# Part of the w2 gradient made between two passes: eight row blocks taken out of the background work of pass 4

## The chip, the cores and the metric

The kernel runs on one core of one Trainium2 chip. The metric is device time in microseconds (us); the program is one launch with one core, so the slowest core is that core. The time before is the median of three runs. The profile is of one further execution, which has its own time.

## The reference

Two layers of a decoder step are applied twice with the same weights: attention of one query token over a long key and value cache (A), then a dense layer with a squared relu (B). The kernel computes the output and its gradient with respect to the nine inputs but `B_x`. All tensors are bf16.

```python
# A: x is (1, 1, 1024); caches (1, 4, 65536, 128); wq (1024, 4096); wo (4096, 1024)
q = (x @ wq) as 32 heads of 128;  8 heads share one of 4 cache groups
p = softmax(q . k * 128**-0.5);   o = p . v;   return o @ wo
# B: w1 (1024, 3584), w2 (3584, 1024)
h = x @ w1 + b1;  r = max(h, 0);  g = r * r;  return g @ w2 + b2

x = x + A(layernorm(x));  x = x + B(layernorm(x))      # layers 1 and 2
x = x + A(layernorm(x));  x = x + B(layernorm(x))      # layers 3 and 4
out, vjp = jax.vjp(f, A_x, A_k_cache, A_v_cache, A_wq, A_wo, B_w1, B_b1, B_w2, B_b2)
return out, *vjp(grad_out)
```

There is only one token, so each weight gradient is a sum of two outer products, one per use of the weight. The gradient of w2 (`out_8`, 3584 x 1024) is

```python
grad_w2 = outer(L4.g, grad_out) + outer(L2.g, dx2)     # rank 2
```

where `L4.g` and `L2.g` are the squared relus of layers 4 and 2 and `dx2` is the gradient that reaches the output of layer 2. It is 28 row blocks of 128 rows.

## The kernel before, in words

**Passes.** The two caches are 64 MB each and are read in four passes: pass 1 (forward of layer 1), pass 2 (forward of layer 3), pass 3 (first backward of layer 3: its dq), pass 4 (both layers' gradients of k and v and the dq of layer 1). In the code they are `attn_fwd` with 0 and 1, `attn_bwd3` with 2 and `attn_bwd4` with 3. A pass is a list of items in `ITEMS`, 256 in each, each 8 columns of 128 cache rows of one of the four groups. `pipeline` (L846) runs its stages over the items with fixed lags. In pass 4 the stages `vT` and `vS` (transposes of v, scores L1390, product L1411) run up to 16 iterations ahead of the others, so its first 16 iterations hold only them.

**The arena.** `ARENA` is one SBUF tile of 20 granules of 1 MB (`GRAN`, L268). Eight of them hold the exponentials of the two forward passes during pass 3 and the start of pass 4. The other twelve are handed out by `take_one` (L292) when a `Slot` is made: cache halves of 1 MB (`kv8`, L351), weight slabs (`slabs`, L441) and output staging all come from there. Free granules carry the time at which they were given back; outside of pass 4 a request takes the one that has been free for longest, or, for output staging, the latest one that has been free for a pipeline step. A slot that was given back with `stored=True` counts as free five steps later. In pass 4 some granules are a ring, `RING`, for output staging; loads take granules outside of it. `xs` is a slot in which pass 4 keeps the products X of its first group, one half of 32 columns in each eighth, the last eighth first. Pass 3 keeps seven turned v halves for pass 4.

**Queues.** All loads go out on SP's queue (L361, L366, L458) and all stores on POOL's. An instruction that reuses a granule waits until the transfer or the engines that used it are done. PE, DVE and ACT run their instructions in the order in which the program lists them inside `tc.manual_schedule` (the turn is such a block); elsewhere, and between these instructions, the scheduler that builds the program orders them.

**The turn between pass 3 and pass 4** (L1854 to L1965). Four matrix-vector products follow from each other: `dn_job` (the last group through wq, gives `dx2`), `dh_job` (through w2, gives `dh2`), `dx_job` (through w1, gives `dx1`) and `do_job` (the first group of pass 4 through wo, gives dO). `rows.tra` turns a weight tile on PE (L688) and evicts it with ACT (kind `kta`) or DVE (`kt`); `rows.back` (L715) multiplies the turned tiles with the vector (L722); `rows.dot` does a tile on DVE instead (L677). `wo_part` turns four of the eight wo rows; it is called once ahead of the last `back` of `dx_job` and once inside its finish. The turned wo rows are written over the slab. When the last `back` of a job is done, `did` runs the job's finish; `dO_finish` (L952) makes the numbers with which the first scores of pass 4 start. Before, nothing of any weight gradient is made here.

**PSUM.** Up to here the pool `psA` has `ps_tr` (three buffers), `ps_sc` (two), `ps_mv`, `ps_bg` and `ps_acc`. Pass 4 opens `ps4`, where `ps_gg` (two buffers of 1024 columns) is for the outer products, and `ps_sc` has one buffer.

**The weight gradients** are background work of pass 4. `Background.step` (L792) is called once an iteration and advances the oldest generator in `bg.normal` by one step whenever `bg.done` is behind `bg.total * i / bg.steps`. `i` counts from the end of the 16 iterations ahead, and is 0 in these. The first generator is `g_outer` (L1537) for w2. Its first step turns the two columns of the right side into two rows (`rows2`, L1489); then, for each four row blocks, one step makes the rows of the left side and four steps make 128x1024 results with `rank2` (L1506) into a staging slot `og`, which is stored as 1 MB behind the last.

`evac` (L150) evicts PSUM with ACT or DVE; for kinds `f32` and `bf` it takes the engine that its running counters find less loaded, and the counters start at zero at pass 4.

Of the kernel before, what the change touches and what calls it, by code (L numbers as in the profile page):

```python
# [16 lines left out]
P = 128  # L17
# [3 lines left out]
def kernel(  # L21
# [24 lines left out]
    nc = tc.nc  # L46
# [47 lines left out]
    def ps_gg():  # L94
        return PS["pool"].tile([P, 1024], F32, name="ps_gg", tag="gg", bufs=2)
# [336 lines left out]
    def d_cols(ap, nb):  # L432
        return ap[:, nb * P:(nb + 1) * P]
# [1052 lines left out]

    def rows2(cols, halves, rows, f=False):  # L1489

        cc = tmp.tile([P, 2, 4, 2], BF, name="r2_cc")
        pg = ps_gg()
        for h, j0 in enumerate(halves):
            for l in range(2):
                nc.vector.tensor_copy(out=cc[:, h, :, l], in_=cols[l][:, j0:j0 + 4])  # L1495
            for jj in range(4):
                nc.tensor.matmul(pg[64 * h:64 * h + 2, jj * P:(jj + 1) * P], lhsT=cc[:, h, jj, :], rhs=ident_b[:, :],  # L1497
                                 start=True, stop=True, tile_position=(0, 64 * h))
        for h in range(len(halves)):
            r = slice(64 * h, 64 * h + 2)  # L1500
            if f:
                evac(rows[r, :].rearrange("r (p j) -> r p j", j=4), pg[r, 0:512].rearrange("r (j p) -> r p j", j=4), kind="f32")
            else:
                evac(rows[r, :], pg[r, 0:512], kind="f32")

    def rank2(out, lhs, rhs):  # L1506

        n = out.shape[1]
        pg = ps_gg()
        for h in range(n // 512):  # L1510
            r = slice(64 * h, 64 * h + 2)
            nc.tensor.matmul(pg[:, 512 * h:512 * h + 512], lhsT=lhs(r), rhs=rhs(r), start=True, stop=True, tile_position=(64 * h, 0))  # L1512
        evac(out, pg[:, 0:n], kind="f32")

    def g_outer_last(pool, out_dram, a_cols, b_cols, c0):

# [17 lines left out]
                yield  # L1534
            sl.free(stored=True)

    def g_outer(pool, out_dram, nA, nB, a_cols, b_cols, c0=0, a_f=False):  # L1537

        rb = pool.tile([66, 4 * P], BF, name="rowb", tag="rowb")
        rows2(b_cols, (0, 4), rb)  # L1540
        yield
        for a0 in range(0, nA, 4):
            ra = pool.tile([66, 4 * P], BF, name="rowa", tag="rowa", bufs=2)
            rows2(a_cols, (a0, a0), ra)
            yield
            sl = Slot("og", True)
            og = sl.t[:, :].rearrange("p (j n) -> p j n", j=4)
            for j in range(4):
                rank2(og[:, j, :], lambda r: d_cols(ra[r, :], j) if a_f else f_cols(ra[r, :], j), lambda r: rb[r, :])
                if j < 3:  # L1550
                    yield
            nc.gpsimd.dma_start(out=out_dram[a0 * P:(a0 + 4) * P, c0:c0 + 1024].rearrange("(p j) n -> p j n", j=4), in_=og)
            sl.free(stored=True)
            yield

# [501 lines left out]
```

## Time and profile before

| | us |
|---|---|
| median of three runs | 1936.69 (1935.64 to 1938.51) |
| the profiled execution | 1936.17 |
| its span in the profile | 1934.3 |
| DMA: bytes and mean rate over the span | 787.62 MB, 407 GB/s |
| of these: loads on SP's queue, stores on POOL's | 617.65 MB, 165.70 MB |
| the turn in the trace: last wq issue to the end of dO | 1095 to 1172 |
| pass 4 in the trace | 1171 to 1934 |

The profile's page gives each engine's busy time, then the span in 40 slices with a digit for the busy tenths of each engine and of the 16 DMA engines. The windows give the same for stretches of one's own choice, the granted PE clock, the share of the DMA engines that was busy and the bytes that they moved. A DMA issue in the timeline is the moment at which the queue handed the transfer over, not its end. A wait names the instruction that stood, the one that released it, and how long the engine had nothing to do; in the lists of waits this is the total, the count and the longest.

### The profile page before, as it was taken

What the parts mean: (1) busy time and instruction counts of PE and PEld (TensorE: products, weight loads), DVE (VectorE), ACT (ScalarE), POOL (GpSimd) and SP (SyncE); (2) the same over time, 40 slices, a digit from 0 to 9 for tenths busy, and PEclk for the clock granted to TensorE, in tenths of its full rate; (3) what the DMA queues carried; (4) which work ended last, traced back from release to release, by engine and by line L of the source; (5) the groups of instructions that cost most, each with busy time, mean ns of one, the idle gap of its engine ahead of it and who ended that gap; (6) DMA issues with size and microseconds to landing.
All of it is one profiled execution on the core that took longest, in us unless ns stands there. A gap on an engine that the chain in (4) does not pass through costs nothing. (4 is left out here: it accounts for less than half of the span.)

```text
span 1934.3 us, 66768 instructions
## 1 busy us (share of the span) xinstructions
PE 1576.4 (81%) x30099; PEld 1292.1 (67%) x30099; DVE 1172.2 (61%) x2448; ACT 1043.8 (54%) x1619; POOL 142.4 (7%) x325
## 2 busy tenths in 40 slices
PE   6878778678878878978787878888996987787977
PEld 6878777678777878867677875555654554454544
DVE  5645555255555554645464576777876886676766
ACT  3434334245333535446363465766876785576765
POOL 0000000000000000000000002111211211121211
PEclk9989999799999988998999999898988998798997
DMA  9999999999999999999999997999999999899998
GB/s 393 427 427 424 429 428 416 399 420 412 428 425 428 428 422 330 379 425 429 426 420 426 405 348 298 425 420 387 424 424 413 420 425 423 349 423 397 425 422 321
DMA packets 107148, 787.62 MB, mean 407 GB/s; under 512 B 9440, under 2 KB 16622, under 8 KB 42222
## 3 DMA queue, kind: packets, MB, share of 16 engines
q1 hardware_dynamic: 82782, 617.65, 77.3%
q0 software_dynamic: 24080, 165.70, 20.5%
q8 instruction: 235, 3.85, 0.7%
q14 instruction: 51, 0.42, 0.1%
HBM read 617.62 MB, written 165.69 MB: 405 GB/s over the span
## 5 line engine op out<-in xcount | busy, mean ns | idle before, releaser
L164 DVE COPY kt<-ps_tr 128x1024 bf16<-128x1024 bf16 x736 | 505.8, 688 | 427.1 <-PE ps_tr L1030 239.5
L161 ACT CAST arena<-ps_gg 128x1024 bf16<-128x1024 f32 x457 | 444.2, 1011 | 183.2 <-PE ps_gg L1434 132.4
L1030 PE MATMUL ps_tr<-ident_b,arena 128*128 128x128 bf16 x3840 | 308.4, 225 | 48.0 <-DMA arena<-in_A_k_cache_dram 35.3
L161 ACT COPY kt<-ps_tr 128x1024 bf16<-128x1024 bf16 x180 | 188.6, 1054 | 184.5 <-PE ps_tr L1224 107.2
L164 DVE CAST arena<-ps_gg 128x1024 bf16<-128x1024 f32 (+2 forms) x186 | 222.4, 1196 | 80.1 <-PE ps_gg L1434 36.0
L1030 PEld LDWEIGHTS <-arena 128*128 128x128 bf16 x3840 | 231.8, 101 | 56.7 <-DMA arena<-in_A_k_cache_dram 37.8
L1434 PE MATMUL ps_gg<-GG,xt 64*128 64x512 bf16 x1024 | 209.8, 408 | 51.2 <-DVE arena L164 36.7
L1131 PE MATMUL ps_acc<-arena 128*128 128x64 bf16 (+4 forms) x4096 | 204.6, 197 | 46.1 <-DMA arena<-in_A_v_cache_dram 33.7
L1048 PE MATMUL ps_sc<-L_qpad,kt 128*128 128x64 bf16 (+7 forms) x3584 | 182.6, 194 | 23.1 <-issue 11.7
L1353 PE MATMUL ps_tr<-ident_b,arena 128*128 128x128 bf16 x1824 | 178.1, 232 | 28.5 <-DMA arena<-in_A_v_cache_dram 25.7
L1113 ACT ACTIVATE arena<-S_sb,L_negm 128x128 bf16<-128x128 f32 x256 | 165.3, 1006 | 57.2 <-DVE L_negm L1098 43.6
L1224 PE MATMUL ps_tr<-ident_b,arena 128*128 128x128 bf16 x2032 | 161.7, 224 | 40.6 <-DMA arena<-in_A_v_cache_dram 39.1
L1131 PEld LDWEIGHTS <-arena 128*128 128x128 bf16 x4096 | 160.0, 101 | 52.1 <-DMA arena<-in_A_v_cache_dram 37.7
L1353 PEld LDWEIGHTS <-arena 128*128 128x128 bf16 x1824 | 117.6, 103 | 84.7 <-issue 54.2
L1048 PEld LDWEIGHTS <-kt 128*128 128x128 bf16 x3584 | 152.0, 100 | 27.3 <-issue 12.8
L1224 PEld LDWEIGHTS <-arena 128*128 128x128 bf16 x2032 | 122.6, 100 | 46.0 <-DMA arena<-in_A_v_cache_dram 41.7
L1465 PEld LDWEIGHTS <-arena 128*128 128x128 bf16 x2048 | 92.4, 101 | 56.4 <-issue 38.5
L1434 PEld LDWEIGHTS <-xt 64*128 64x128 bf16 x1024 | 64.4, 94 | 97.8 <-issue 60.2
L1113 ACT ACTIVATION_READ_ACCUMULATOR arena<-S_sb,L_negm 128x1 f32 x256 | 128.2, 501 | 0.0
L584 ACT ACTIVATE mv_t<-mv_t 128x1024 bf16<-128x1024 bf16 x96 | 102.0, 1064 | 43.0 <-DVE mv_t L595 42.8
L1278 PE MATMUL ps_acc<-dsT,arena 128*128 128x64 bf16 (+7 forms) x2048 | 102.4, 194 | 12.4 <-DMA arena<-in_A_k_cache_dram 7.2
L1390 PE MATMUL ps_sc<-DOB,kt 128*128 128x64 bf16 (+3 forms) x1824 | 112.3, 197 | 0.1
(319 smaller groups left out, 2104.3 us busy)
## 6 DMA issues: line engine op xcount, KB each, us to landing
arena<-in_A_k_cache_dram SPq DMA_DIRECT2D x82, 2048.0 KB, 21.3
arena<-in_A_v_cache_dram SPq DMA_DIRECT2D x79, 2048.0 KB, 20.1
out_dram<-arena POOLq DMA_DIRECT2D x149, 1024.0 KB, 15.6
arena<-in_A_v_cache_dram SPq DMA_DIRECT2D x84, 1024.0 KB, 13.1
arena<-in_A_k_cache_dram SPq DMA_DIRECT2D x84, 1024.0 KB, 14.6
arena<-in_A_wo_dram SPq DMA_DIRECT2D x22, 1024.0 KB, 14.9
arena<-in_B_w_dram SPq DMA_DIRECT2D x21, 1024.0 KB, 10.0
arena<-in_A_wq_dram SPq DMA_DIRECT2D x18, 1024.0 KB, 13.4
```

The costliest lines, as they stand in the source:

```text
L161: nc.scalar.copy(out=out, in_=in_)
L164: nc.vector.tensor_copy(out=out, in_=in_)
L584: nc.scalar.activation(out=t[:, :], in_=t[:, :], func=ACTF.Copy, accum_out=y[:, kc:kc + 1])
L1030: nc.tensor.transpose(pt[:, i, :], kb8[:, i, :], ident_b[:, :])
L1048: nc.tensor.matmul(state["ps_s"][:, s:s + w, :].rearrange("p a b -> p (a b)"), lhsT=kt[:, i, :], rhs=L["qpad"][:, g, 0:w, :].rearrange("p ...
L1113: nc.scalar.activation(out=E(p, g, c0, SU)[:, :, h], in_=S[:, h, :], func=ACTF.Exp, bias=L["negm"][:, g, su, h:h + 1], scale=SCALE, accum_ ...
L1131: nc.tensor.matmul(ps_o[:, 0:w, :], lhsT=vb8[:, i, :], rhs=E(p, g, c, w), start=(c % SU == 0), stop=(c % SU == SU - 1), skip_group_check=True)
L1224: nc.tensor.transpose(pt[:, i, :], vb8[:, i, :], ident_b[:, :])
L1278: nc.tensor.matmul(ps_dq[:, 0:w, :].rearrange("p a b -> p (a b)"), lhsT=kb8[:, i, :], rhs=dsT[:, s:s + w, :].rearrange("p a b -> p (a b)") ...
L1353: nc.tensor.transpose(pt[:, i, :], vb8[:, i, :], ident_b[:, :])
L1390: nc.tensor.matmul(state["ps_dp"][:, s:s + w, :].rearrange("p a b -> p (a b)"), lhsT=vt[:, i, :], rhs=DOB[:, g, 0:w, :].rearrange("p a b - ...
L1434: nc.tensor.matmul(pg[:, 512 * h:512 * h + 512], lhsT=xt[64 * h:64 * h + 64, j1 // 8 + m, :], rhs=gg[64 * h:64 * h + 64, :, :].rearrange(" ...
```

## The change

The generator for w2 is split at row block 8. A generator `early` with the first eight row blocks is made in the turn, and the background's one starts at block 8. `early` has 11 steps: the right side's rows, then twice the left side's rows and four results. Two steps stand behind the first `wo_part`, ahead of the last `back` of `dx_job`; two inside `dO_finish`, one at each of its yields; the other seven behind `do_job`. It stages in two arena slots and stores each in two halves.

`rows2` and `rank2` work outside of pass 4 too: there they use `ps_sc` tiles of 512 columns in place of `ps_gg`, so a 128x1024 result is two evictions, all on ACT (`kta`), and the small casts of `rows2` run on POOL in place of DVE. In pass 4 they do what they did.

The background's count starts at -8, so that eight steps are due at once, in the iterations ahead of pass 4's other stages, and its total is smaller by the early work.

```diff
-    def rows2(cols, halves, rows, f=False):
+    def rows2(cols, halves, rows, f=False, kind="f32"):
         cc = tmp.tile([P, 2, 4, 2], BF, name="r2_cc")
-        pg = ps_gg()
+        pg = ps_gg() if PS["pass4"] else ps_sc([P, 512])
+        cast = nc.vector if PS["pass4"] else nc.gpsimd
...
-                nc.vector.tensor_copy(out=cc[:, h, :, l], in_=cols[l][:, j0:j0 + 4])
+                cast.tensor_copy(out=cc[:, h, :, l], in_=cols[l][:, j0:j0 + 4])
...
-                evac(rows[r, :], pg[r, 0:512], kind="f32")
-    def rank2(out, lhs, rhs):
+                evac(rows[r, :], pg[r, 0:512], kind=kind)
+    def rank2(out, lhs, rhs, kind="f32"):
         n = out.shape[1]
-        pg = ps_gg()
-        for h in range(n // 512):
-            r = slice(64 * h, 64 * h + 2)
-            nc.tensor.matmul(pg[:, 512 * h:512 * h + 512], ...)
-        evac(out, pg[:, 0:n], kind="f32")
+        step = n if PS["pass4"] else 512
+        for n0 in range(0, n, step):
+            pg = ps_gg() if PS["pass4"] else ps_sc([P, 512])
+            for h in range(n0 // 512, (n0 + step) // 512):
+                r = slice(64 * h, 64 * h + 2)
+                nc.tensor.matmul(pg[:, 512 * h - n0:512 * h + 512 - n0], ...)
+            evac(out[:, n0:n0 + step], pg[:, 0:step], kind=kind)
...
-    def g_outer(pool, out_dram, nA, nB, a_cols, b_cols, c0=0, a_f=False):
+    def g_outer(pool, out_dram, nA, nB, a_cols, b_cols, c0=0, a_f=False, start=0, kind="f32"):
...
-        for a0 in range(0, nA, 4):
+        for a0 in range(start, nA, 4):
...
             for j in range(4):
-                rank2(og[:, j, :], ..., lambda r: rb[r, :])
+                rank2(og[:, j, :], ..., lambda r: rb[r, :], kind)
+                if PS["pass4"]:
+                    if j == 3:
+                        nc.gpsimd.dma_start(out=rows, in_=og)
+                elif j % 2:
+                    nc.gpsimd.dma_start(out=rows[:, j - 1:j + 1, :], in_=og[:, j - 1:j + 1, :])
                 if j < 3:
                     yield
-            nc.gpsimd.dma_start(out=out_dram[...], in_=og)
             sl.free(stored=True)
             yield
...
-    do_job = rows.job(R, DC, lambda: dx1[:], dO_finish(L1, firstg[3]))
+    def fin_dO(y):
+        for _ in dO_finish(L1, firstg[3])(y):
+            next(early, None)
+            yield
+    EARLY = 8
+    early = g_outer(DENSE["pool"], out_8, EARLY, DC, [L4["g"], L2["g"]], [gx, dx2], a_f=True, kind="kta")
+    do_job = rows.job(R, DC, lambda: dx1[:], fin_dO)
...
         wo_part()
+        next(early)
+        next(early)
         while rows.queue[0][0] is dx_job:
             rows.back()
         rows.begin(do_job)
         while rows.queue:
             rows.back()
         next(wo_it, None)
+        run(early)
...
-    bg.normal.append(g_outer(bgpool, out_8, FC, DC, [L4["g"], L2["g"]], [gx, dx2], a_f=True))
+    bg.normal.append(g_outer(bgpool, out_8, FC, DC, [L4["g"], L2["g"]], [gx, dx2], a_f=True, start=EARLY))
...
-    bg.total = 2 + n_outer(FC, DC) + n_outer(DC, FC, True) + n_outer(HQ, DC) + (G - 1) * n_outer(DC, DC)
+    bg.done = -8
+    bg.total = 2 + n_outer(FC - EARLY, DC) - 8 + n_outer(DC, FC, True) + n_outer(HQ, DC) + (G - 1) * n_outer(DC, DC)
```

More of the change, by code (lines that the diff above doesn't have):

```diff
@@ L1503, in rows2 @@
             else:
-                evac(rows[r, :], pg[r, 0:512], kind="f32")
-    def rank2(out, lhs, rhs):
+                evac(rows[r, :], pg[r, 0:512], kind=kind)
+    def rank2(out, lhs, rhs, kind="f32"):
         n = out.shape[1]
-        pg = ps_gg()
-        for h in range(n // 512):
-            r = slice(64 * h, 64 * h + 2)
-            nc.tensor.matmul(pg[:, 512 * h:512 * h + 512], lhsT=lhs(r), rhs=rhs(r), start=True, stop=True, tile_position=(64 * h, 0))
-        evac(out, pg[:, 0:n], kind="f32")
+        step = n if PS["pass4"] else 512
[3 more added lines that the diff above has]
+                r = slice(64 * h, 64 * h + 2)
+                nc.tensor.matmul(pg[:, 512 * h - n0:512 * h + 512 - n0], lhsT=lhs(r), rhs=rhs(r), start=True, stop=True,
+                                 tile_position=(64 * h, 0))
+            evac(out[:, n0:n0 + step], pg[:, 0:step], kind=kind)
     def g_outer_last(pool, out_dram, a_cols, b_cols, c0):
@@ L1535, in g_outer_last @@
             sl.free(stored=True)
-    def g_outer(pool, out_dram, nA, nB, a_cols, b_cols, c0=0, a_f=False):
+    def g_outer(pool, out_dram, nA, nB, a_cols, b_cols, c0=0, a_f=False, start=0, kind="f32"):
         rb = pool.tile([66, 4 * P], BF, name="rowb", tag="rowb")
-        rows2(b_cols, (0, 4), rb)
+        rows2(b_cols, (0, 4), rb, kind=kind)
         yield
-        for a0 in range(0, nA, 4):
+        for a0 in range(start, nA, 4):
             ra = pool.tile([66, 4 * P], BF, name="rowa", tag="rowa", bufs=2)
-            rows2(a_cols, (a0, a0), ra)
+            rows2(a_cols, (a0, a0), ra, kind=kind)
             yield
@@ L1547, in g_outer @@
             og = sl.t[:, :].rearrange("p (j n) -> p j n", j=4)
+            rows = out_dram[a0 * P:(a0 + 4) * P, c0:c0 + 1024].rearrange("(p j) n -> p j n", j=4)
             for j in range(4):
-                rank2(og[:, j, :], lambda r: d_cols(ra[r, :], j) if a_f else f_cols(ra[r, :], j), lambda r: rb[r, :])
+                rank2(og[:, j, :], lambda r: d_cols(ra[r, :], j) if a_f else f_cols(ra[r, :], j), lambda r: rb[r, :], kind)
+                if PS["pass4"]:
[3 more added lines that the diff above has]
+                    nc.gpsimd.dma_start(out=rows[:, j - 1:j + 1, :], in_=og[:, j - 1:j + 1, :])
                 if j < 3:
                     yield
-            nc.gpsimd.dma_start(out=out_dram[a0 * P:(a0 + 4) * P, c0:c0 + 1024].rearrange("(p j) n -> p j n", j=4), in_=og)
             sl.free(stored=True)
```

## The prediction

> **What bounds the kernel now.** I read the page's slices first, then the windows around the turn, then the SP queue and the waits there. The page says what the whole kernel is short of:
>
> ```profile
> span 1934.3 us, 66768 instructions
> PE 1576.4 (81%) x30099; PEld 1292.1 (67%) x30099; DVE 1172.2 (61%) x2448; ACT 1043.8 (54%) x1619; POOL 142.4 (7%) x325
> DMA  9999999999999999999999997999999999899998
> ```
>
> The DMA row (40 slices of 48.4 us) is full nearly everywhere; only slice 25, from 1160 to 1209 us, falls to 7. 50 us windows of pass 4 mostly show 418 to 425 GB/s at a share of 1.00 or 1.01. So a transfer moved out of pass 4 is worth its bytes only if it lands where the DMA engines are idle. The windows of 5 us show where that is (columns: busy time of PE, PEld, DVE, ACT and POOL, PE clock, DMA share, GB/s):
>
> ```profile
> 1160.00:1165.00 5.00, 3.76 (x78) 3.76 (x78) 3.06 (x8) 3.09 (x5) 0.61 (x1) 1.00 1.06 431
> 1165.00:1170.00 5.00, 3.17 (x81) 2.96 (x78) 2.57 (x12) 1.46 (x2) 0.68 (x1) 1.00 0.43 174
> 1170.00:1175.00 5.00, 4.26 (x100) 3.36 (x101) 4.27 (x27) 2.13 (x4) 1.17 (x5) 1.00 0.40 118
> 1175.00:1180.00 5.00, 4.23 (x89) 2.74 (x84) 2.09 (x8) 3.70 (x5) 0.85 (x1) 1.00 1.01 362
> 1185.00:1190.00 5.00, 3.97 (x47) 2.29 (x47) 2.35 (x5) 2.25 (x4) 1.15 (x2) 1.00 0.58 243
> 1190.00:1195.00 5.00, 3.83 (x34) 1.88 (x33) 3.01 (x4) 2.18 (x3) 0.53 (x1) 0.60 0.50 211
> ```
>
> Two holes. The first, 1165 to 1175, is worth (0.57 + 0.60) x 5 = 5.85 us; windows of 1 us put it between 1167 and 1174. The second, 1185 to 1195, is worth (0.42 + 0.50) x 5 = 4.6 us. Why they are there is in the SP queue: every slot is taken, and the next load waits for one.
>
> ```profile
> 1156.28 16.04 SPq L361 DMA_DIRECT2D arena<-in_A_k_cache_dram  x3
> 1174.68 0.33 SPq L361 DMA_DIRECT2D arena<-in_A_v_cache_dram  x1
> 1177.71 0.33 SPq L361 DMA_DIRECT2D arena<-in_A_k_cache_dram  x1
> 1179.88 0.33 SPq L361 DMA_DIRECT2D arena<-in_A_v_cache_dram  x1
> 1195.92 0.33 SPq L458 DMA_DIRECT2D arena<-in_A_wo_dram  x1
> ```
>
> The first row is pass 4's first two k loads (1156.28 and, by a narrower window, 1157.5) and a third at 1172.00; a load shows on the DMA engines 1.3 us after its issue (1172.00 to 1173.3). The third k and the next three are each released when the scores L1390 of one kept v half are done. The wo load waits for a later kept half. Between 1180 and 1196 compute feeds the DMA engines with stores alone. The end of the kernel moves with the idle time of the DMA engines, so I count that, up to the wo load.
>
> **What is moved.** Eight blocks are 1024 rows of 2 KB: 2.1 MB, 4.95 us at 424 GB/s. More is drawn forward by `bg.done = -8`: eight background steps run in pass 4's 16 lead iterations, where none ran. When the wo load of 1195.92 goes out, at iteration 32, the old kernel (`bg.total` 150 over 252 iterations) had done 16 x 150/252 = 9.5 steps and stored one 1 MB slot. The new one has done the 11 early steps and 8 + 16 x 132/252 = 16, that is two early slots and three more. Four slots more are stored by then: 9.9 us of DMA work.
>
> **What the k loads lose.** The two early slots are taken from the free ones by age, before pass 4 asks. By `take_one` they are the two granules that the sixth and seventh w1 slab leave, which the first two k loads have now. The k loads get the next: the eighth w1 slab's, free when its last dot ends at 1160.75, and that of the first wo slab, free when the first four `back` of `do_job` are done (about 1168.9, and later as below). So the first k goes out at 1160.8 and runs from 1162.1 to 1164.6 (1.05 MB at 424 GB/s is 2.5 us); the second goes out at 1170.3 instead of 1157.5 and starts at 1171.6. Idle up to 1171.6 is 7.3 us, where the 1 us windows of before add up to 4.4: **+2.9 us**. No early store can fill this hole: the outer products come behind `do_job`.
>
> **What the chain to dO loses.** Two `rows2` stand ahead of the last `back` of `dx_job`. PE: 2 x 0.40 us (L1497 x8). The second needs the `ps_sc` buffer that the fourth wo transposes filled, and DVE empties it at 1163.24 to 1163.93, so these `back` start at 1164.4 instead of 1163.0: 1.4 us later. ACT: 4 evictions of 2x512 at 0.58 us, 2.3 us; they push the wo evictions of 1164.53 and 1165.44 to an end near 1168.8, still ahead of `do_job` at 1167.8 + 1.4. The casts go to POOL (the trace's nearest is L1333's 128x128, 0.30 us), which is idle from 1142 to 1164, and wait for nothing of the turn: nothing if they run there, 8 x 0.30 = 2.4 us if not.
>
> **What the start of pass 4 loses.** The early slices are 16 evictions of 128x512 on ACT at 0.59 us and two of 2x512: 10.6 us from 1171.8. ACT's idle time from 1171.5 to 1196 is 11 us by the windows. The two further slots (about 5 us of the work falls to ACT, since `evac` shares it with DVE but knows nothing of the early load) bring it to 15.6 us, so iteration 32 comes at least 4.6 us late; not below 0, since nothing else in that stretch becomes shorter.
>
> There is also a wait. `xs` takes the oldest granule outside the ring, which is now the first early slot. Its first X product (L1411, 1172.52) writes the last eighth, which the second half store still reads. This store is issued after 8 evictions, near 1176.8. The nearest landing is that of the last stores:
>
> ```profile
> out_dram<-arena POOLq DMA_DIRECT2D x4, 512.0 KB, 3.1
> ```
>
> So X starts near 1180 instead of 1172.5. Queued behind it on DVE are whatever the schedule put there, on PE the next half's scores (`ps_sc` has one buffer in pass 4), and on SP the v, k and v loads of 1174.68 to 1179.88. Seven halves at the 2.2 us that the second to fifth take (1177.72, 1179.88, 1182.05) end near 1195, about where they do now, if DVE and PE are free. Bounds for the delay S of iteration 32 are thus 2 and 14 us; I take 7, near what ACT alone asks.
>
> **The sum.** After 1171.6 the idle time of before is 10.2 - 4.4 = 5.8 us (1 us windows: 5.9 in the first hole, 4.3 in the second). The new kernel has 9.9 us of stores and the late k load, 2.5 us, to put there: 12.4. The hole closes, and opens again by what S exceeds 12.4 - 5.8 = 6.6 us. So the change is +2.9 - 5.8 + (7 - 6.6), about **-2.5 us**. With S up to 6.6 it is -2.9. Later in pass 4 the background falls from 0.595 to 0.524 steps an item; this is free of effect while the DMA engines are full, and the holes after 1200 (8.5 us up to 1900, the largest 6.3 us at 1665 to 1680, behind a DVE wait of 14.4 us on a wq slab) can each come or go when the order of instructions shifts. I give that no sign and 4 us either way. The profiled execution took 1936.17 us beside its span of 1934.3, the median of three is 1936.69: I predict 1934.3. About 0.2%, 3.9 us, is what a measurement of this kernel can tell from no change, so this is inside it.
>
> **Rival one, faster.** The late k load costs nothing, because the chain to dO has slack in it, ACT catches up and all 5 us of moved stores come off pass 4, with some of the later holes closing as its ACT and DVE work falls by 11 steps of about 1.1 us: 1936.2 - 5 - 1 = about 1930. For it: the second hole is real, and DVE and ACT together are idle 20 us between 1171.5 and 1196. Against it: the k loads are on the queue ahead of everything else and their granules are settled by the program.
>
> **Rival two, slower.** The store waits decide. Before, both evicting engines already stood once for a store to leave a slot:
>
> ```profile
> DVE arena L164 <- DMA out_dram<-arena: 2.4, 1, 2.4
> ACT arena L161 <- DMA out_dram<-arena: 1.7, 1, 1.7
> ```
>
> Now four fills of the start follow a store: X behind the first early one, the fourth slot of the gradient behind the second, the first dV slot behind the third, the first dK slot as before. If X's 7.5 us are not caught up, two more waits cost 2.4 each, and the chain's 1.4 comes on top, S is 13.7; with the 2.5 us by which X waits longer if the store shares the engines with the k loads (a 1 MB store issued at 1182.28 freed its slot at 1189.9) it is 16. Then the change is -2.9 + (16 - 6.6) = +6.5, less what ACT's overlap hides: about 1942. It is slower than before from S = 9.5 on, and measurably so from 13.4. For it: all these engines take their work in order. Against it: S of 13 means that DVE, idle half of that stretch, recovers nothing.
>
> [...]
>
> **A third.** The schedule puts early PE and ACT work ahead of pass 4's first scores instead of between them: scores from 1171 to 1182, S above 10, and a time like rival two's.
>
> **Chances.** The sum's own case 0.46, its range 1930 to 1938.5, with 0.16 of it below 1932.8, 0.24 within, 0.06 above. Rival one 0.20 (all but 0.02 faster). Rivals two and three 0.34 (0.32 slower). That makes faster 0.34, same 0.28, slower 0.38. The range reaches to 1928 for rival one and 1943 for rival two.
>
> **What would show it.** Right: an idle DMA stretch from about 1165 to 1171.6, then none of over 2 us before 1200; first k issues near 1161 and 1170; four stores of 512 KB issued between 1175 and 1185; X's first product waiting for DMA near 1180; 22 early ACT evictions near 0.59 us; the wo load near 1203. Wrong: k loads as early as now, a wo load past 1209, or the second hole back at full size. If these all come as said and the time is still off by over 4 us, the step that failed is that the rest of pass 4 keeps its holes.

## The result, and the profile after

The changed kernel is slower: 1960.59 us, the median of six runs (1955.31 to 1965.27), against 1935.88 us before, the median of six (1929.03 to 1938.51). The ratio is 1.0124, 95% interval 1.0107 to 1.0142, that is +24.0 us (20.7 to 27.5). The forecast was 1934.3 with a range from 1928 to 1943; the measured time lies outside it, on the slower side. The profiled execution of the changed kernel took 1965.27 us, the longest of its six, beside 1936.17 for that of before; it lies 5 us above its median.

From the page of the changed kernel:

```profile
span 1963.5 us, 66793 instructions
PE 1599.8 (81%) x30107; PEld 1303.0 (66%) x30107; DVE 1168.5 (60%) x2434; ACT 1051.3 (54%) x1635; POOL 148.0 (8%) x339
DMA  9999999999999999999999977999999999999995
```

PE has 23 us more busy time with eight instructions more, at a mean granted clock of 0.907 against 0.920; no other engine has gained more than 8 us. The DMA row now has two slices at 7 (1129 to 1227) where there was one, and a 5 at the end. The windows of 5 us, with the same columns as before:

```profile
1165.00:1170.00 5.00, 4.54 (x92) 4.07 (x88) 3.60 (x15) 4.93 (x8) 1.12 (x5) 1.00 0.63 218
1170.00:1175.00 5.00, 3.34 (x67) 2.81 (x68) 1.94 (x10) 0.70 (x1) 0.12 (x1) 0.79 0.22 43
1175.00:1180.00 5.00, 3.98 (x16) 1.09 (x16) 1.17 (x11) 4.29 (x8) 1.16 (x3) 0.50 0.67 272
1180.00:1185.00 5.00, 4.06 (x9) 0.69 (x8) 0.39 (x4) 4.62 (x8) 1.06 (x2) 0.50 0.27 108
1185.00:1190.00 5.00, 4.31 (x52) 2.75 (x50) 2.79 (x13) 2.26 (x5) 1.15 (x2) 0.50 0.51 210
1190.00:1195.00 5.00, 5.00 (x42) 2.17 (x43) 3.77 (x8) 2.49 (x3) 0.53 (x2) 0.50 0.65 210
1195.00:1200.00 5.00, 4.98 (x83) 3.59 (x80) 3.10 (x9) 2.56 (x4) 1.76 (x3) 0.83 0.41 170
```

Between 1165 and 1200 the DMA share falls short of 1 by 18.2 us (0.37 + 0.78 + 0.33 + 0.73 + 0.49 + 0.35 + 0.59, times 5); before, it was 10.5. The holes were to be filled and have become larger. From 1175 to 1185 PE issues 25 matmuls where before there were 174: only the early gradient runs. The timeline of PE (start, duration, in brackets the idle time before and what ended it) shows what waits for it:

```profile
1174.39 0.60 PE L1515 MATMUL ps_sc<-rowb,rowa 2*128 2x512 bf16 x2
...
1180.71 4.96 PE L1515 MATMUL ps_sc<-rowb,rowa 2*128 2x512 bf16 x8 [0.69 <-ACT rowa L161]
1186.35 1.03 PE L1498 MATMUL ps_gg<-ident_b,r_cc 128*2 128x128 bf16 x16 [0.67 <-ACT arena L161]
1187.30 1.73 PE L1390 MATMUL ps_sc<-DOB,arena 128*128 128x64 bf16 x29
1188.96 0.60 PE L1515 MATMUL ps_gg<-rowb,rowa 2*128 2x512 bf16 x1
```

L1515 is the product of `rank2`, L1498 that of `rows2`, L1390 the scores. The first line of L1498 on `ps_gg`, pass 4's own PSUM, is released by ACT's last eviction of the early gradient; it is the front-loaded background step, and only behind it come the first scores, 12.3 us after dO. The next background product stands again between the scores. Before, the scores came 0.4 us after dO, released by a small instruction of DVE that belongs to dO:

```profile
1170.36 0.16 DVE L1317 TENSOR_TENSOR CCf<-L_dOT,L_rZ 128x8 f32<-128x8 f32 x1
1170.90 1.07 PE L1390 MATMUL ps_sc<-DOB,arena 128*128 128x64 bf16 x32 [0.25 <-DVE negd L962]
```

(dO is counted here and below from the end of L1317, the last DVE instruction that takes the new `dOT`, 0.35 us behind the end of its write at L954.) On SP's queue, in the changed kernel, the loads follow:

```profile
1163.95 36.48 SPq L361 DMA_DIRECT2D arena<-in_A_k_cache_dram  x4
1201.28 1.32 SPq L361 DMA_DIRECT2D arena<-in_A_v_cache_dram  x2
1207.00 0.33 SPq L458 DMA_DIRECT2D arena<-in_A_wo_dram  x1
```

The first v load went out at 1174.68 before and does so at 1201.28 now. Waits for stores have grown too (list of waits, 1160 to 1225: total, count, longest; before, 2.4 and 1.7):

```profile
ACT arena L161 <- DMA out_dram<-arena: 8.6, 1, 8.6
DVE arena L164 <- DMA out_dram<-arena: 6.0, 1, 6.0
PE ps_gg L1434 <- DVE arena L164: 5.2, 1, 5.2
```

The delay stays: the seventh X product is 23.2 us later than before and the last of the 64 is 20.9 us later. The end is 29.2 us later in these two executions, because another 8.3 us are lost behind the last X product. No experiment here looks at these, and how many of the other executions lose them is not known.

### The profile page after: what moved, and what is told of

Its sections match the earlier page's. It is cut to its first block, busy times and chain, and to the rows that moved or that the text cites. A ratio compares the mean times of both kernels' runs of the same rounds, so it can differ in the third digit from the quotient of the medians.

```text
span 1963.5 us, 66793 instructions
## 1 busy us (share of the span) xinstructions
PE 1599.8 (81%) x30107; PEld 1303.0 (66%) x30107; DVE 1168.5 (60%) x2434; ACT 1051.3 (54%) x1635; POOL 148.0 (8%) x339
## 5 line engine op out<-in xcount | busy, mean ns | idle before, releaser
L161 ACT CAST arena<-ps_gg 128x1024 bf16<-128x1024 f32 (+1 forms) x450 | 437.6, 1012 | 195.3 <-PE ps_gg L1434 125.8
L1048 PEld LDWEIGHTS <-kt 128*128 128x128 bf16 x3584 | 152.1, 100 | 26.7 <-issue 14.0
L1465 PEld LDWEIGHTS <-arena 128*128 128x128 bf16 x2048 | 94.0, 103 | 71.3 <-issue 46.7
L1390 PEld LDWEIGHTS <-kt 128*128 128x128 bf16 x1824 | 83.5, 102 | 48.0 <-issue 47.3
L1390 PE MATMUL ps_sc<-DOB,kt 128*128 128x64 bf16 (+3 forms) x1824 | 114.4, 198 | 0.0
## 6 DMA issues: line engine op xcount, KB each, us to landing
arena<-in_A_k_cache_dram SPq DMA_DIRECT2D x82, 2048.0 KB, 20.7
arena<-in_A_v_cache_dram SPq DMA_DIRECT2D x84, 1024.0 KB, 12.6
```

The lines of the kernel that those rows point to most:

```text
L161: nc.scalar.copy(out=out, in_=in_)
L1048: nc.tensor.matmul(state["ps_s"][:, s:s + w, :].rearrange("p a b -> p (a b)"), lhsT=kt[:, i, :], rhs=L["qpad"][:, g, 0:w, :].rearrange("p ...
L1390: nc.tensor.matmul(state["ps_dp"][:, s:s + w, :].rearrange("p a b -> p (a b)"), lhsT=vt[:, i, :], rhs=DOB[:, g, 0:w, :].rearrange("p a b - ...
L1465: nc.tensor.matmul(ps_dq[:, 0:w, :].rearrange("p a b -> p (a b)"), lhsT=kb8[:, i, :], rhs=X[:, s:s + w, :].rearrange("p a b -> p (a b)"), ...
```

## The experiments

Two parts can be separated: the early gradient in the turn, and `bg.done = -8`, the front-loading. Differences to before are from the ratio of the runs beside each other, with its 95% interval; the expectations quote differences of medians, which are up to 2 us off these.

| label | what it is | us against before |
|---|---|---|
| (the change) | early gradient and front-loading | +24.0 (20.7 to 27.5) |
| early_only | early gradient alone | +8.1 (5.8 to 10.5) |
| early4_only | the same, four row blocks | +6.2 (4.1 to 8.5) |
| early_two | the same, ACT and DVE evict in turn | +8.1 (5.4 to 10.6) |
| dummy_barrier | no gradient, 16 evictions that nobody reads | +9.7 (6.2 to 13.2) |
| lead_only | front-loading alone | +18.0 (13.9 to 22.1) |
| lead_newest | the same, another granule for the v load | +20.7 (14.9 to 26.3) |
| lead6 | six steps instead of eight | +9.3 (5.8 to 12.8) |
| all_lead | sixteen steps | +22.5 (17.8 to 27.3) |
| early4 | the change with four row blocks | +12.8 (8.3 to 17.2) |
| lead_pause | eight steps in the lead, then none until pace | +10.8 (6.8 to 14.9) |
| lead_late | the same, in lead iterations 8 to 15 | +4.6 (1.5 to 7.6) |
| surplus_only | nothing in the lead, eight steps ahead behind it | +8.3 (5.2 to 11.4) |
| mid8 | eight steps more in iterations 100 to 107 | -0.2 (-2.9 to 2.5) |
| lag8 | eight steps less at the start | +6.6 (3.7 to 9.5) |
| lag8_catch, lag16_catch | eight, sixteen less, made up in the middle | +1.2 (-1.4 to 3.7), -0.4 (-2.7 to 2.1) |
| after_late | the change, steps in lead iterations 8 to 15 | +13.4 (9.5 to 17.2) |

For the start of pass 4, from one profiled execution each, all in us: from the end of the wo load to dO (the end of L1317), and from there to the first scores and the seventh X product (L1411). The execution that was profiled is not always a typical one: those of lead6 (1937.83), lead_late (1935.21), surplus_only (1941.56) and lag8 (1938.43) are among the fastest of their kernels, that of after_late (1965.33) is the slowest.

| | wo to dO | dO to scores | dO to 7th X |
|---|---|---|---|
| before | 6.8 | 0.4 | 25.7 |
| the change | 8.6 | 12.3 | 44.4 |
| early_only | 8.5 | 11.3 | 40.1 |
| early4_only | 10.4 | 4.9 | 37.5 |
| dummy_barrier | 7.7 | 9.1 | 33.4 |
| lead_only | 8.1 | 1.0 | 32.3 |
| lead_pause | 6.8 | 0.9 | 37.6 |
| lead_late | 8.4 | 0.4 | 26.3 |
| surplus_only | 7.5 | 0.4 | 25.8 |

**Taking the change apart.** early_only drops the front-loading:

```diff
-    bg.done = -8
-    bg.total = 2 + n_outer(FC - EARLY, DC) - 8 + ...
+    bg.total = 2 + n_outer(FC - EARLY, DC) + ...
```

> The changed kernel without its front-loading: bg.done stays 0 and the total is not lowered by 8, so no background step runs in the 16 lead iterations. The early gradient in the turn stays. Theory A (barrier): pass 4 opens all eight PSUM banks, and so its first scores wait until the last early result is evicted; the early work behind do_job is in series with pass 4, and the delay stays to the end. Then first scores L1390 stay near 1187 (before: 1170.9), the lead steps' share (about 4 us at the second X) is saved, and the kernel is at +14 to +20 us against before, 1950 to 1956. Theory B (granules: late k loads and a v load on a granule whose store is pending): the same granules are taken, so +20 to +25, as the changed kernel. Theory C (the front-loaded background steps alone): within 4 us of before.

lead_only is the kernel before with

```diff
-    bg.total = 2 + n_outer(FC, DC) + ...
+    bg.done = -8
+    bg.total = 2 + n_outer(FC, DC) - 8 + ...
```

> The kernel before with the front-loading alone: bg.done = -8 and the total lowered by 8; no early gradient. Theory A: the first scores start as before (1171) since nothing of the turn is left in PSUM; eight steps of about 1.1 us share ACT and DVE with scores that have slack: 0 to +4 us. Theory B: the v load is put on a granule with its store pending here too, so +5 to +10 us. Theory C: most of the loss, +18 to +25 us.

early4 is the change with `EARLY = 4`.

> The changed kernel with four early row blocks in place of eight: one early slot, and behind do_job only four results (8 evictions of 128x512 at 0.59 us, less than half of the 16 and a turning of rows). Theory A: the barrier shrinks by about 6 us, first scores near 1180.5 to 1181.5 and the kernel 5 to 9 us faster than the changed kernel, 1951 to 1956. Theory B: one granule less is taken, so the first k load is as early as before and the time falls by 10 or more, to below 1950, with the first scores where A puts them. Theory C: no change against the changed kernel.

all_lead is lead_only with -16 in both places.

> The kernel before with 16 background steps drawn forward (bg.done = -16, the total lowered by 16) and nothing in the turn: three slots of the gradient are made in pass 4's lead, in the same PSUM pool as the scores. Theory A: without the barrier as much work as in the changed kernel costs little, -4 to +6 us against before; the first scores stay near 1171. Theory C: worse than the eight steps of the changed kernel, +25 us or more. Theory B: between, +5 to +12 us from slots taken from the ring early.

The first theory (A, the barrier carries nearly all) fell: the front-loading alone costs twice what the early gradient does, and the two together (26.1) make up the 24.0. That they add up is in part chance: in the profiled executions the changed kernel is 20.9 us late at the last X product, where lead_only is 23.4 and early_only 7.0, and the 8.3 us behind it bring it near their sum. C has lead_only right but not early_only, which it put within 4 us of before; B falls with early_only, where it had +20 to +25. The 22.5 us of all_lead lie between what B and C gave: twice the steps cost little more than eight. Of A the place stands: the first scores come 11.3 us after dO in early_only and 1.0 in lead_only. Four blocks save 11 us of the change's 24, more than the 6.4 us by which the scores come earlier in early4_only than in early_only.

**Is it the granule?** The rule for the first loads of pass 4 takes the granule that was freed latest, and with the front-loading this is the slot whose store has just been issued. lead_newest is lead_only with

```diff
-            i = by_age[-1][1]
+            i = [i for t, i in by_age if t <= NOW["step"]][-1]
```

> The kernel before with the front-loading alone (bg.done = -8), and the load rule of pass 4's start mended: the newest free granule is taken only among those whose time has come, so that the first v load goes to the v half freed by the scores (as before) and not onto the slot whose 1 MB store has just been issued. The front-loading alone cost +19.7 us. Theory F (granule): that pick is the cause; then 0 to +6 us against before, first v load near 1176 to 1180 instead of 1187. Theory G (occupation): the eight steps stand between the scores on PE, ACT and DVE and put off everything behind them, whatever granule is taken; +14 to +20 us. Theory H (half slot): the second slot, begun and left half full through the lead, takes the ring's last granule; +14 to +20 us too.

lead6 has -6 in place of -8, so that no second slot is begun in the lead.

> The kernel before with six steps drawn forward instead of eight (bg.done = -6, total lowered by 6): one slot made and stored, no second one begun in the lead. The v load still falls onto the slot being stored. Theory F: +15 to +20 us, as with eight. Theory G: three quarters of it, +12 to +16. Theory H: +2 to +8.

Theory F is out: the first v load went out at 1180.0 (1187.2 in lead_only), and the time did not fall. lead6 lies between what G and H gave: half of the cost goes with the last two steps. Its ten runs spread from 1937.8 to 1955.6.

**Is it the barrier?** Without the front-loading: early4_only has `EARLY = 4`, early_two evicts half of the early results with DVE:

```diff
-            evac(out[:, n0:n0 + step], pg[:, 0:step], kind=kind)
+            evac(out[:, n0:n0 + step], pg[:, 0:step], kind=kind if PS["pass4"] else ("kta", "kt")[n0 // 512 % 2])
```

> Four early row blocks and no front-loading. With eight the early part alone cost +8.2 us. Theory A (barrier: pass 4's PSUM pool opens only when the last early result is evicted): the work behind do_job falls from 16 evictions and a turning of rows to about 6 evictions, 7 us less, so +0 to +4 us. Theory K (the early slots push the k loads onto later granules): half of the slots, so about +4 to +7, with the third k load as late as with eight.

> Eight early row blocks, no front-loading, and the early results evicted by ACT and DVE in turn instead of ACT alone: the same slots, loads and stores, only the time between dO and pass 4's first scores is shorter, by about 4 to 5 us. Theory A: +3 to +5 us against before. Theory K: no change, +7 to +9.

early_two did not do what it was made for: the scores came 11.9 us after dO, not earlier, because PE, whose clock was 0.62 from 1170 to 1175 and 0.50 from 1175 to 1185, was as slow as the evictions (five products in 3.11 us). It says nothing on A. early4_only brought the scores forward to 4.9 us, as A had it, but the time by only 2 us: in its profile dO was 3.6 us later behind the wo load than before, and the seventh X product only 2.6 us earlier than with eight blocks. So the barrier was made by itself, in the kernel before:

```diff
         while rows.queue:
             rows.back()
         next(wo_it, None)
+        for _ in range(16):
+            pg = ps_sc([P, 512])
+            junk = mvs.tile([P, 1024], BF, name="mv_junk", tag="mv_t", bufs=2)
+            nc.tensor.matmul(pg[:, :], lhsT=ident_b[:, :], rhs=dx_job["room"][:, 0:512], start=True, stop=True)
+            evac(junk[:, 0:512], pg[:, :], kind="kta")
```

> The kernel before with a barrier and nothing else: behind do_job PE writes 16 ps_sc tiles of 128x512 and ACT evicts each into a scratch tile that nobody reads. It takes no arena slot, stores nothing, moves no work; ACT's time behind dO is that of the early gradient (16 x 0.59 = 9.4 us). Theory A (barrier): the first scores start 9 to 11 us after dO instead of 0.4, and the kernel is 8 to 11 us slower than before, as or a little more than the early part alone (+8.6), which also took 5 us of stores out of pass 4. Theory K (the early slots push the k loads onto later granules): -1 to +2 us.

It cost 9.7 us, and A holds for the early part. PE's timeline (L1967 is the added product) and the windows:

```profile
1177.27 0.86 PE L1967 MATMUL ps_sc<-w_vbc,ident_b 128*128 128x512 bf16 x2 [0.18 <-ACT mv_junk L161]
1178.81 1.07 PE L1390 MATMUL ps_sc<-DOB,arena 128*128 128x64 bf16 x32 [0.67 <-ACT mv_junk L161]
```

```profile
1165.00:1170.00 5.00, 3.58 (x67) 3.31 (x68) 1.38 (x10) 0.00 (x0) 0.00 (x0) 0.67 0.12 50
1170.00:1175.00 5.00, 3.53 (x10) 0.86 (x9) 1.06 (x10) 4.66 (x9) 0.59 (x2) 0.99 0.01 3
1175.00:1180.00 5.00, 3.45 (x39) 1.63 (x38) 0.73 (x3) 3.76 (x8) 0.61 (x1) 1.00 0.00 0
```

No byte and no slot has moved, yet the DMA engines stand still from 1170 to 1180, because the loads that would run there wait for scores. The scores are released by the last eviction of tiles that have nothing to do with them: the program lists them for PE behind the products of these tiles, and opens pass 4's PSUM pool where `psA` was. The last wait, 0.67 us, is for the eviction; which of the two sets the rest was not tried apart. Scores that come 9.6 us later behind the wo load (0.9 + 8.7) cost 9.7. In early_only they come 12.6 us later (1.7 + 10.9) and cost 8.1, in early_two 12.7 and 8.1, in early4_only 8.1 and 6.2. Less the time of the bytes that these kernels no longer store in pass 4 (4.95 us by the prediction's estimate, half of it for four blocks), the delays are 7.7, 7.8 and 5.6 us. So all four fit one estimate, the delay of the scores less the time of the moved stores; single executions and intervals of 2 to 4 us to either side allow no more than that.

**The front-loading's two halves.** lead_pause runs eight steps in the lead and then stands still until the old pace has reached them; surplus_only runs none in the lead and is granted the eight steps behind it:

```diff
 # lead_pause, with bg.floor = 8
-            while self.normal and self.done < self.total * i / self.steps:
+            while self.normal and self.done < max(self.floor, self.total * i / self.steps):
 # surplus_only, with bg.extra = 8 and the total lowered by 8
+            if i > 0 and self.extra:
+                self.done -= self.extra
+                self.extra = 0
```

> The kernel before with the same eight steps drawn into the lead, but without a lasting surplus: the background then stands still until the old pace (150 steps over 252 iterations) has caught up with them, at iteration 14 behind the lead. Theory G (occupation of the lead): the steps among the first scores cost, +14 to +20 us, as the front-loading alone (+19.7). Theory S (surplus: eight steps, that is more than one slot, ahead of pace until the pass's end, so that stores and ring slots press on the loads when the kept v halves run out): 0 to +5 us.

> The complement of the last: nothing runs in the lead, and the surplus of eight steps is granted at the first iteration behind it (total lowered by 8), so that the background runs at one step an iteration from there until it is eight steps ahead of pace. Theory S: +14 to +20 us. Theory G: 0 to +5 us.

Neither theory has it alone: 10.8 and 8.3, together 19.1 beside lead_only's 18.0. What the lead's half is shows beside lead_late, where the same steps start eight iterations later:

```diff
+            self.calls += 1
-            while self.normal and self.done < self.total * i / self.steps:
+            while self.normal and self.done < max(8 if PS["pass4"] and self.calls > 8 else 0, self.total * i / self.steps):
```

> As lead_pause (+11.8 us: eight steps in the lead, no lasting surplus), but the steps stand in lead iterations 8 to 15 instead of 0 to 7, behind the scores that release the third k load. If the cost is the late release of that load (1174 instead of 1172, with the DMA engines idle from 1170 to 1176): 0 to +5 us. If it is the compute of eight steps in a stretch bound by compute (theory C): +8 to +12 us. Theory R: +7 to +9.

4.6 us remain, in the late load's range. PE in lead_pause (there L1513 is `rank2`, L1391 the scores), then SP's queue in lead_pause and in lead_late:

```profile
1169.96 1.02 PE L1391 MATMUL ps_sc<-DOB,arena 128*128 128x64 bf16 x29
...
1175.26 0.60 PE L1513 MATMUL ps_gg<-rowb,rowa 2*128 2x512 bf16 x2
1175.79 0.77 PE L1391 MATMUL ps_sc<-DOB,arena 128*128 128x64 bf16 x11
1176.49 0.61 PE L1513 MATMUL ps_gg<-rowb,rowa 2*128 2x512 bf16 x2
```

```profile
1154.95 30.13 SPq L361 DMA_DIRECT2D arena<-in_A_k_cache_dram  x4
1185.25 2.06 SPq L361 DMA_DIRECT2D arena<-in_A_v_cache_dram  x2
```

```profile
1154.12 17.91 SPq L361 DMA_DIRECT2D arena<-in_A_k_cache_dram  x3
1174.38 0.33 SPq L361 DMA_DIRECT2D arena<-in_A_v_cache_dram  x1
1177.64 0.33 SPq L361 DMA_DIRECT2D arena<-in_A_k_cache_dram  x1
```

The steps stand between the scores on PE. Scores that are finished later release granules later (from 1150 to 1192 the loads' queue waited twice for scores in lead_pause, 26.9 us in all, and once before, 14.2), and the first v load goes out 16.2 us after dO instead of 4.2. With the steps eight iterations further back it is 4.2 again, and the seventh X product is where it was (26.3 against 25.7, lead_pause 37.6). But lead_late's twelve runs spread from 1933.8 to 1947.0, and the profiled one was no slower than before; where the 4.6 us go its trace does not show.

The other half shows 60 to 130 us later, in PE's waits for a k half (stretch 1200 to 1300; surplus_only, then before; L1469 and L1465 are the same line):

```profile
PE ps_acc L1469 <- DMA arena<-in_A_k_cache_dram: 16.7, 3, 8.5
```

```profile
PE ps_acc L1465 <- DMA arena<-in_A_k_cache_dram: 4.6, 2, 4.5
```

The same stretch has 16.9 in lead_newest, 14.4 in lead_only, 11.2 in lead6, 10.7 in early4 and 8.3 in the changed kernel, all with a lasting surplus; without one, before, early_only, early_two, early4_only, dummy_barrier, lead_pause, lead_late and mid8 have 4.0 to 6.7. Two kernels with the surplus are exceptions: after_late has 6.1, and all_lead 0.9, but from 1185 to 1300 26.2 us of waits for stores. In lead_only 12.3 us fall in one piece. The only k load then under way was issued at 1257.52, and the product that waited started at 1277.34. Before it on the queue stood five loads issued since 1242, and the stores of six slots went out between 1242 and 1264. The load is 2.5 us of traffic by itself (the prediction's estimate), and 19.8 us passed from its issue to the product. From 1258 to 1277 the DMA engines moved 3.35 MB for the loads' queue and 4.04 MB for the stores'; the loads had less than half of the bytes, and how the engines divide their time between the two was not shown. Behind that wait the DMA share fell to 0.14 (1275 to 1280): between 1263.6 and 1282.5 no load and no store was issued. Why the surplus makes the k loads late there and, by mid8 below, not further on is not settled.

**Would any shift do that?** lag8 goes the other way:

```diff
+    bg.done = 8
-    bg.total = 2 + n_outer(FC, DC) + ...
+    bg.total = 2 + n_outer(FC, DC) + 8 + ...
```

> The opposite sign: the background starts eight steps behind (bg.done = 8, total raised by 8), so none of it runs in the first 13 iterations behind the lead, and it makes this good over the pass. Theory S: the same press taken away, so the kernel is faster than before, by 3 to 10 us. Theory G: the lead is as before; -2 to +2 us.

It was slower by 6.6. In its profile, of the fastest of its ten runs, nearly all X products from the seventh on are earlier behind dO than before, the last by 6.1 us, but from the last k product (L1465) to the end it takes 26.6 us instead of 19.2: steps were left over for the end (32 of the 184 matmuls of `rank2` come behind the last X product, before 22). Three kernels ask whether the place or the mere shift matters. The `_catch` kernels are lag8, with 8 or 16, and

```diff
                 if r == "wait":
                     break
+                if PS["pass4"] and i >= 60 and self.done < self.total * i / self.steps - 6:
+                    break
                 return
```

> The background eight steps behind at the start, as in lag8; but from iteration 60 on, while it is more than six steps behind pace, it may make a step in an iteration in which urgent work ran too, so that none is left for the tail (lag8 left seven of them there). Theory C (the start is bound by compute, the middle by DMA): the 6 us that lag8 was ahead through the pass stay, so 3 to 8 us faster than before. Theory R (any shift disturbs): +4 to +9 us.

> The same with sixteen steps. Theory C: as lag8_catch or up to 5 us better, as long as the start is compute-bound for that long (sixteen steps are those of the first 27 iterations). Theory R: +4 to +10 us.

mid8 is the kernel before with

```diff
         def step(self, i):
+            if PS["pass4"] and 100 <= i < 108:
+                next(self.normal[0])
+                self.done += 1
```

> The kernel before with eight additional steps forced into iterations 100 to 107, where the DMA engines are full (share 1.01); the start is untouched, and later the pace falls behind by less. Theory C: -3 to +3 us against before, since their compute lies beside full DMA engines. Theory R: +5 to +9 us, as the same surplus at iteration 1 (+8.3).

R is out: eight steps more in the middle of the pass cost nothing (-0.2). By the 28th X product mid8 has made 98 matmuls of `rank2` against 88, as far ahead as surplus_only is at the eighth (22 against 12). Shifts of eight or sixteen steps the other way leave the time as it was if they are made up before the end. C holds for steps added: they cost at the start and not where the DMA engines are full. It fails for steps taken away: lag8_catch is ahead of before for nearly all of the stretch from the seventh to the 46th X product (the 45th by 8.7 us), and then mostly behind (the 64th by 3.2). Whether the catching up costs it or something at the end of the pass is open, and no kernel here beats the one before.

**Back in the changed kernel.** after_late is the change with the eight steps in lead iterations 8 to 15:

```diff
-            while self.normal and self.done < self.total * i / self.steps:
+            while self.normal and self.done < (-8 if PS["pass4"] and self.calls <= 8 else self.total * i / self.steps):
```

> The changed kernel with its eight front-loaded steps in lead iterations 8 to 15 instead of 0 to 7; early gradient, slots and surplus as they are. If the place ahead of the first scores costs here what it cost in the kernel before (11.8 - 4.7 = 7.1 us), the kernel is 7 us faster than the changed one: about +17 against before, 1952 to 1955. If the scores' lateness behind the barrier already hides it: no change, 1958 to 1962.

+13.4 instead of +24.0, 10.6 us less: the place of these steps costs in the changed kernel what it costs alone (10.8 - 4.6 = 6.2), or somewhat more; the intervals do not tell these apart.

## Why the prediction was wrong

**What bounds it.** The DMA engines were read as the limit, and their idle time as room that bytes could fill. At the start of pass 4 they are idle because compute has not yet freed the granules: dummy_barrier leaves them idle for ten microseconds there (share 0.01 and 0.00 from 1170 to 1180) without moving a byte. In the sum a delay S costs only what exceeds 6.6 us, because 12.4 us of transfers were to move into 5.8 us of idle time. That way of counting holds where it could be tried: dummy_barrier moves no transfer, so all of its 9.6 us of delay should count, and it cost 9.7 (6.2 to 13.2). What failed are two terms that were put in: S itself, and the half of the moved stores that the front-loading was to bring.

**What is moved, one of the two steps that failed.** Four slots more by iteration 32, 9.9 us, was the credit. Two of the slots are the early ones; their 4.95 us came back, as far as the estimate above goes (early_only, early_two). The two others were to come from the front-loading, which stored no more: from 1180 to 1250 the trace of lead_only has 13 stores of a slot, that of before 14, two more for the weight gradient and three fewer for the caches' gradients. This credit was a cost of 18 us. Part of that cost falls behind the wo load, where the sum put nothing but 4 us either way: surplus_only has the seventh X product on time (25.8 against 25.7) and the twelfth 14.5 us late, and costs 8.3. How the surplus delays the loads is open.

**The late k loads.** First k issues were put at 1160.8 and 1170.3; they came at 1163.95 and 1172.91, in an execution that was already 1.75 us late at the turn's first dense weights (1110.98 against 1109.23) and 2.7 at the wo loads (1155.29 against 1152.61). The granules were as said. The DMA engines' idle time up to the second k load is 5.5 us in windows of 1 us (1164 to 1174), not 7.3. Whether the +2.9 by itself is right no run shows: the barrier leaves the DMA engines idle there anyway.

**The chain to dO.** +1.4 was forecast; 1.8 measured in the change, 1.7 in early_only. The place is as forecast: the last `back` of `dx_job` start 3.07 us behind the first wo transposes in both, 1.80 before, with the second `rows2` right ahead of them. But the same stretch to dO is 1.3 us longer in lead_only and 1.6 in lead_late, whose turn is that of before, so the size is not shown.

**The start of pass 4, the other step that failed.** The work was sized rightly: 10.4 us of ACT for the early evictions (10.6 forecast), 0.53 to 0.59 each, and four half stores at 1177.66, 1180.15, 1184.08 and 1186.59 (forecast 1175 to 1185). Its place was wrong: it was taken to lie beside the scores, so that ACT's idle time there paid for most of it; it lies ahead of them. S, taken as 7 between 2 and 14, is 18.7 at the seventh X product. It grows from 11.9 at the scores; in early_only, without front-loaded steps but at the same low PE clock (0.50 from 1170 to 1180), from 10.9 to 14.4, and in dummy_barrier, at full clock (0.99 and 1.00 from 1170 to 1180), not at all (8.7, then 7.7). What the clock costs was not tried apart. With 18.7 in place of 7 the sum gives +9.2 (2.9 - 12.4 + 18.7). That, the lost credit of 4.95 and the 8.3 behind the wo load make 22.5 of the 24.0; this is an estimate over several kernels. The marker chosen for it, the wo load, came at 1207.0, ahead of the 1209 that was to show the forecast wrong, and misled: it waits for another granule than before. The other marker, the second hole back at full size, did appear. X did not wait for its half store. It started at 1190.33, released by PE, with the last half store landed at 1189.4; so the 2.5 us that rival two put on that wait no run shows.

**The rivals.** The third, early work ahead of the first scores, is what happened. It put the scores at 1182; they began at 1187.3, behind ACT's last early eviction and a front-loaded step. Its 1942 was too low, since it gave the front-loading the same credit and put nothing behind the wo load. Rival two's store waits did appear (8.6 and 6.0 us); how much of the loss they carry was not tried. That eight background steps at the head of the pass might cost more than their own time (18.0 us against 8 x 1.1) was no rival at all.

## What to carry to other kernels

An idle DMA stretch is only room for bytes if the loads behind it are not waiting for compute: look at what releases the next load, and treat every instruction that is put ahead of that releaser as a delay of the whole pass. Work that is moved out of a stage must also be followed into the pool that the next stage opens, since tiles of the old one can stand ahead of its first work up to their last eviction: in dummy_barrier the first scores came 9.1 us after dO. Where a background step costs nothing in the middle of a pass (mid8, -0.2 us for eight), the same step among the first instructions can cost more than its own time (lead_only, 18.0 us for eight of about 1.1).

## What the runs showed of the hardware

In the two stretches that follow, PE's granted clock did not follow PE's busy share. In the changed kernel it was 0.50 from 1175 to 1185 with PE busy for 0.80 and 0.81 of the time, mostly on products with two rows of operands (`2*128 2x512`); in dummy_barrier it was 0.99 and 1.00 from 1170 to 1180 with PE busy for 0.71 and 0.69, up to 1178 on products with 128 rows (`128*128 128x512`). The pace was similar, two products every 1.25 us in the one and every 1.05 in the other. In dummy_barrier the clock had been 0.67 in the window from 1165 to 1170, and the first of these products started at 1169.80; in early_two it was 1.00 from 1165 to 1170, where those of two rows began at 1169.26, then 0.62 up to 1175 and 0.50 up to 1185. At 0.50 a product of two rows took 0.58 us, in before at 1.00 0.38, and the scores that followed still ran at 0.50: 29 matmuls in 1.73 us, where dummy_barrier does 32 in 1.07. Busy time at the low clock is longer for the same work, so the two shares are not quite alike. What set the clock in either kernel was not shown; the number of rows was not tried by itself.
